# A gated layer's gate and value evacuated over 512 columns, and its input's transposing transfers begun on SyncE

## The chip, the cores and the metric

The kernel runs on one core of a Trainium2 chip. The metric is the time of one execution on the device, in microseconds (us). Times inside an execution are counted from the start of the profiled span.

## What is computed

Three layers, one after the other, over 4 x 768 tokens of 384 features (8 heads of 48):

```python
for t in range(S):                                   # attention with a decaying state
    y[:, :, t] = einsum('bhd,bhde->bhe', rt, state + einsum('bhd,bhe->bhde', u * kt, vt))
    state = wt[:, :, :, None] * state + einsum('bhd,bhe->bhde', kt, vt)
x = y.transpose(0, 2, 1, 3).reshape(B * S, H * D)    # 3072 x 384
x = (1 / (1 + exp(-(x @ w_gate))) * (x @ w_val)) @ w_out      # gated layer, width 1536
h = x @ w_in
return (h * tanh(log1p(exp(h)))) @ w_out2                     # width 2048
```

## The kernel before

All matmuls of the two layers run in half precision with each operand split in a high and a low part, three products for one (high by high, high by low, low by high). Weights come from memory as 64-bit words and are decoded on the chip (`decode`, `decode_early`) into those two parts.

The tokens go in 12 pairs of attention steps, p = 0 to 11, each a block of 256 tokens (`NT`); step j = 2p + e makes one half of a block. `step(j)` computes the attention's rows on TensorE (tile `yp`, L728), splits them into high and low (`xs`, lines 212 and 215) and brings them, turned, into `xt[p]`, the input of the gated layer. For p = 0 and 1 TensorE turns them (`flip_x`, L747) and ScalarE and VectorE copy them out of PSUM (`put`); from p = 2 on two transposing transfers do it (`send`, L762), begun on ScalarE's queue, one for the high and one for the low part. They make 40 transfers in all.

`gate(p, f)` handles 128 of the 1536 inner features (f = 0 to 11). TensorE makes nine matmuls of 256 columns with the gate weights and nine with the value weights (L880), into the two halves of one PSUM bank (tile `gv`, tags pg0 to pg3; three of them for p = 0, four later). Four steps then evacuate the bank: ScalarE's sigmoid of the gate half (L891), VectorE's product with the value half, in place (L896), ScalarE's high part of it into `gt` (L908), VectorE's rest into `gt` (L911). After the last one the bank is free. `out1(p, c, part)` multiplies the finished `gt` of a block with the output weights (L943), in parts that are strewn among the gates of the next block; its result `xo` goes to memory (`x2d`, L979) and is read back for the second layer (`h`, L1053; `o`, L1168), which begins after the last block.

The order of work on every engine is a planner's. Each piece is added with its engine, an estimated cost in us, what it reads and what it writes; the planner computes a latest start for each from the end back, walks forward taking on each engine the ready piece with the earliest latest start, and writes the program in the order of the planned begins. Engines then run their own lists in that order and wait on semaphores. On TensorE the gates come in the order of p and f; attention's matmuls go in between. SyncE's list holds the loads of raw weights (L267), of `blk` (L449) and `v` (L471) for attention, the stores of `x2d` (L979) and the loads of `x2` (L1032).

The lines that carry the four steps' planned costs before are these:

```python
        add("act", 0.34, sigmoid, [ps, "table1"], [sg])
        add("dve", 0.35, product, [sg], [ps])
        ...
            add("act", 0.34, high, [ps, *room], [(*G, 0)])
        ...
        add("dve", 0.35, rest, [ps, (*G, 0)], [(*G, 1)])
```

Of the kernel before, what the change touches and what calls it, by code (L numbers as in the profile page):

```python
# [7 lines left out]
F32 = mybir.dt.float32  # L8
# [3 lines left out]
AF = mybir.ActivationFunctionType  # L12
# [19 lines left out]
NT = 256  # L32
# [3 lines left out]
SW = 256.0  # L36
SX = 64.0
# [8 lines left out]
COLD = 1.9  # L46
# [17 lines left out]
class Plan:  # L64
# [11 lines left out]
    def add(self, eng, cost, fn, reads=(), writes=(), lat=SEM, burst=False):  # L76
        t = Task()
        t.cost = eng if isinstance(eng, dict) else {eng: cost}
        t.fn, t.lat, t.burst = fn, lat, burst
        t.rank = len(self.tasks)  # L80
        t.deps = set()
        for k in reads:
            if k in self.writer:
                t.deps.add(self.writer[k])
        for k in writes:
            if k in self.writer:
                t.deps.add(self.writer[k])
            t.deps.update(self.readers.pop(k, ()))
        for k in reads:
            self.readers.setdefault(k, []).append(t)  # L90
        for k in writes:
            self.writer[k] = t
        self.tasks.append(t)
# [66 lines left out]
def mixer_moe_kernel(  # L160
# [12 lines left out]
    nc = tc.nc  # L173
    PS = bass.MemoryType.PSUM
    plan = Plan()
    add = plan.add
# [6 lines left out]
    mp = ctx.enter_context(tc.tile_pool(name="mp", bufs=1))  # L183
    pg = ctx.enter_context(tc.tile_pool(name="pg", bufs=1, space=PS))
# [20 lines left out]
    def attn(eng, cost, fn, reads=(), writes=(), lat=SEM, burst=False):  # L205
        add(eng, cost, fn, [*reads, "attention"], writes, lat, burst)
# [51 lines left out]
    def next_pg(n=4):  # L258
        npg[0] += 1
        return ("pg", npg[0] % n)  # L260
# [449 lines left out]
    def step(j):  # L710
        p, e = divmod(j, 2)
# [46 lines left out]
        def send(_):  # L758
            if e == 0:
                new_xt()  # L760
            for i in range(2):
                nc.scalar.dma_start_transpose(  # L762
                    out=xt[p][:, i, :, 128 * e : 128 * e + 128], in_=xss[j][:, i]
                )

# [20 lines left out]
        reads = [(*xs, 0), (*xs, 1)]  # L786
        room = [("xt", p % 2, 0, 0)] * e
        if p < 2:

            tbank = next_at()  # L790
            attn("pe", 0.6, flip_x, [*reads, "eye"], [tbank])
            attn("act", 0.48, lambda on: put(on, 0), [tbank, *room], [("xt", p % 2, e, 0)])
            room = [("xt", p % 2, 0, 0)]
            attn("dve", 0.48, lambda on: put(on, 1), [tbank, *room], [("xt", p % 2, e, 1)])
        else:
            new = [("xt", p % 2, e, i) for i in range(2)]
            attn("act", 0.15, send, [*reads, *room], new, lat=2.8)
        if j + 1 == NJ:
            return

# [47 lines left out]
        cold = COLD if j < 4 else 1.0  # L848
# [8 lines left out]
    gps = {}  # L857
    gt = {}
    sgs = {}
    ops = {}  # L860
    xos = {}
    nsg = [0]
    nxo = [0]
    w2 = {}

    def gate(p, f):
        ps = next_pg(4 if p else 3)
        sg = ("sig", nsg[0] % 3)
        nsg[0] += 1
        G = ("gt", p % 2, f)  # L870
        fs = slice(128 * f, 128 * f + 128)

        def sums(o):
            if o == 0:
                gps[p, f] = pg.tile([128, 2, NT], F32, tag=f"pg{ps[1]}", name=f"gv{p}_{f}")
            w = (wgs, wvs)[o]
            n = 0
            for a, c in ((0, 0), (0, 1), (1, 0)):
                for kc in range(KC):
                    nc.tensor.matmul(  # L880
                        gps[p, f][:, o],
                        w[:, a, kc, fs],
                        xt[p][:, c, kc, :],
                        start=(n == 0),
                        stop=(n == 3 * KC - 1),
                    )
                    n += 1

        def sigmoid(e):
            sgs[p, f] = mp.tile([128, NT], F32, tag=f"sig{sg[1]}", name="sig")  # L890
            nc.scalar.activation(  # L891
                out=sgs[p, f], in_=gps[p, f][:, 0], func=AF.Sigmoid, scale=1.0 / (SW * SX)
            )

        def product(e):
            nc.vector.scalar_tensor_tensor(  # L896
                out=gps[p, f][:, 1],
                in0=gps[p, f][:, 1],
                scalar=SG / (SW * SX),
                in1=sgs.pop((p, f)),  # L900
                op0=ALU.mult,
                op1=ALU.mult,
            )

        def high(e):
            if f == 0:
                gt[p] = mp.tile([128, 2, NF1, NT], F16, tag=f"gt{p % 2}", name=f"gt{p}")
            nc.scalar.copy(out=gt[p][:, 0, f], in_=gps[p, f][:, 1])  # L908

        def rest(e):  # L910
            nc.vector.tensor_tensor(  # L911
                out=gt[p][:, 1, f],
                in0=gps[p, f][:, 1],
                in1=gt[p][:, 0, f],
                op=ALU.subtract,
            )

        x = [("xt", p % 2, e, i) for e in range(2) for i in range(2)]
        for o in range(2):
            w = [(("wg", "wv")[o], f, a) for a in range(2)]  # L920
            cold = COLD if p == 0 and f < 3 else 1.0
            add("pe", 0.99 * cold, lambda e, o=o: sums(o), [*x, *w, "gates"], [ps])
        add("act", 0.34, sigmoid, [ps, "table1"], [sg])
        add("dve", 0.35, product, [sg], [ps])
        room = [("gt", p % 2, "tile")]
        if f:
            add("act", 0.34, high, [ps, *room], [(*G, 0)])
        else:
            add("act", 0.34, high, [ps], [(*G, 0), *room])
        add("dve", 0.35, rest, [ps, (*G, 0)], [(*G, 1)])  # L930

    def out1(p, c, part):
        bank = "po2" if p > NP - 3 and (KC * p + c) % 2 else "po"
        cs = slice(128 * c, 128 * c + 128)
        fr = range(3 * part, 3 * part + 3)

        def sums(e):
            if part == 0:
                pool = w2["po"] if bank == "po2" else po
                ops[p, c] = pool.tile([128, 512], F32, tag="po", name=f"o1{p}_{c}")  # L940
            for f in fr:
                for n, (a, g) in enumerate(((0, 0), (1, 0), (0, 1))):
                    nc.tensor.matmul(  # L943
                        ops[p, c][:, :NT],
                        wos[:, a, f, cs],
                        gt[p][:, g, f, :],
                        start=(f == 0 and n == 0),
                        stop=(f == NF1 - 1 and n == 2),
                    )

        reads = [("gt", p % 2, f, a) for f in fr for a in range(2)]
        reads.append(("gt", p % 2, "tile"))
        reads += [("wo", f // 2, a) for f in fr for a in range(2)]
        if bank == "po2":
            reads.append("open")
        add("pe", 0.99, sums, [*reads, "outs"], [bank])
        if part < 3:
            return
        n = nxo[0]
        nxo[0] += 1  # L960
        xo = ("xo", n % 3)

        def new():
            xos[n] = mp.tile([128, 2, NT], F16, tag=f"xo{n % 3}", name="xo")

        split(
            xo,
            lambda: ops[p, c][:, :NT],
            lambda: xos[n][:, 0],
            lambda: xos[n][:, 1],  # L970
            SX / (SW * SG),
            0.35,
            [bank],
            new,
        )
        add(
            "sp",
            0.4,
            lambda e: nc.sync.dma_start(out=x2d[p, c], in_=xos[n]),  # L979
            [(*xo, 0), (*xo, 1)],  # L980
            [("x2d", p, c)],
            lat=2.0,
        )
# [322 lines left out]
    for p in range(NP):  # L1306
        for f in range(NF1):
            if p + 1 < NP:
                if f == YPOS[0]:
                    tail1(p + 1)  # L1310
                if f == YPOS[1]:
                    tail2(p + 1)
                    if p + 2 < NP:
                        cells[p + 2] = fine(p + 2)
                    else:
                        tail_end()
            if f == 0 and p >= NP - 1:
                load_x2(0)
                load_x2(1)
            gate(p, f)  # L1320
            if p > 0:
                for part in PARTS[f % 4] if p > 2 else [f % 4]:
                    out1(p - 1, f // 4, part)

            if f == 3 and p > 1 and (p + 2, 2) in late:
                late.pop((p + 2, 2))()
            if f == 11 and (p + 3, 1) in late:
                late.pop((p + 3, 1))()
# [73 lines left out]
```

## Time and profile before

| | us |
|---|---|
| median of three runs | 967.01 (963.94 to 968.82) |
| the profiled execution, its own time | 966.59 |
| its span, first to last instruction | 964.9 |
| TensorE busy in the span | 895.1 |
| VectorE busy | 662.0 |
| ScalarE busy | 497.1 |
| GpSimd busy | 490.6 |

The engines are named PE (TensorE matmuls), PEld (its weight loads), DVE (VectorE), ACT (ScalarE), POOL (GpSimd) and SP (SyncE). A q behind an engine's name means its queue, where transfers are issued. L880 is line 880 of the kernel. In a row of a group, the part before the bar names line, engine, operation and tiles; behind it stand busy time, the mean of one instruction, and the idle time of the engine just before, with what ended it.

### The profile page before, as it was taken

To read this page: it belongs to the slowest core of one execution; us is meant where nothing else is said; L and a number is where in the kernel's file an instruction comes from. 1 tells how busy PE (TensorE), PEld (TensorE's weight loads), DVE (VectorE), ACT (ScalarE), POOL (GpSimd) and SP (SyncE) were. 2 spreads that over 40 slices of the span, in tenths; PEclk is the share of its full clock that TensorE was granted. 3 is DMA by queue.
4 is the path that set the end of the run, shared out by engine and by line. 5 is a ranking of instruction groups with operands and counts; after the bars stand their busy time and mean duration, and the time that the engine had idled before them with its cause. 6 is when DMAs were issued, how large, how long until landed. Compare 5 with 4: busy or idle time off the path is not lost.

```text
span 964.9 us, 29600 instructions
## 1 busy us (share of the span) xinstructions
PE 895.1 (93%) x12808; PEld 715.3 (74%) x12808; DVE 662.0 (69%) x1202; ACT 497.1 (52%) x1191; POOL 490.6 (51%) x534
## 2 busy tenths in 40 slices
PE   0567899999999999999999999999999999999998
PEld 0455678888888888888888787657767676776788
DVE  7889976767676857686778798875565655556541
ACT  2757864343525253443436566775565655656540
POOL 7999832626454536546374365654343443444330
PEclk9988899999999999999999999999999999999999
DMA  9445842322232223232222760010100102000000
GB/s 316 143 139 165 261 116 75 67 69 69 68 56 69 75 70 80 49 75 59 61 53 78 190 206 12 8 44 1 37 30 10 58 1 66 2 9 26 1 34 34
DMA packets 56467, 71.92 MB, mean 75 GB/s; under 512 B 20752, under 2 KB 37648, under 8 KB 56208
## 3 DMA queue, kind: packets, MB, share of 16 engines
q1 hardware_dynamic: 39696, 66.09, 23.3%
q10 hardware_dynamic: 16640, 3.94, 2.1%
q8 instruction: 100, 1.64, 0.7%
q14 instruction: 31, 0.25, 0.1%
HBM read 56.64 MB, written 9.44 MB: 68 GB/s over the span
## 4 chain that ended last, share of the span: by engine, by line
PE 71%; DVE 13%; ACT 7%; POOL 4%; ACTq 2%; issue 2%; DMA 1%; SPq 0%; DVEq 0%; POOLq 0%
PE gv L880 20%; PE h L1053 19%; PE o L1168 17%; PE o L943 10%; PE yp L728 3%; ACT X L655 2%; DVE X L655 2%; ACTq L762 2%; ACT KK L697 2%; DVE A L506 1%; PE kp L824 1%; POOL sum_wp L332 1%; PE lp L638 1%; DVE gt L911 1%; POOL pt L486 1%
## 5 line engine op out<-in xcount | busy, mean ns | idle before, releaser
L1053 PE MATMUL h<-x,wis 128*128 128x512 f16 x864 | 199.9, 379 | 1.3 <-DVE gt L911 1.3
L880 PE MATMUL gv<-xt,wgs 128*128 128x256 f16 x1296 | 165.0, 277 | 14.7 <-DVE gt L911 14.1
L486 POOL TENSOR_TENSOR blk<-blk 128x384 f32<-128x384 f32 (+2 forms) x139 | 127.6, 931 | 99.4 <-DMA blk<-rkw 71.7
L943 PE MATMUL o<-gt,wos 128*128 128x256 f16 x1296 | 165.3, 273 | 2.2 <-DVE xo L215 2.0
L1087 POOL TENSOR_TENSOR sum<-e 128x256 f32<-128x256 f32 x96 | 71.6, 746 | 185.8 <-ACT e L1064 185.7
L880 PE MATMUL gv<-xt,wvs 128*128 128x256 f16 x1296 | 163.9, 276 | 1.9 <-DVE wvs L306 1.2
L880 PEld LDWEIGHTS <-wgs 128*128 128x128 f16 x1296 | 125.8, 99 | 33.7 <-issue 15.7
L1053 PEld LDWEIGHTS <-wis 128*128 128x128 f16 x864 | 83.4, 98 | 84.4 <-issue 1.5
L943 PEld LDWEIGHTS <-wos 128*128 128x128 f16 x1296 | 125.9, 98 | 20.6 <-issue 2.9
L880 PEld LDWEIGHTS <-wvs 128*128 128x128 f16 x1296 | 125.1, 99 | 20.4 <-DVE wvs L306 1.5
L486 POOL TENSOR_TENSOR pt<-blk 128x384 f32<-128x384 f32 x93 | 105.5, 1159 | 45.0 <-DMA blk<-rkw 41.7
L891 ACT ACTIVATE sig<-gv 128x256 f32<-128x256 f32 x144 | 53.6, 385 | 118.0 <-PE gv L880 110.5
L1064 ACT ACTIVATE e<-h 128x512 f32<-128x512 f32 x96 | 57.3, 597 | 84.0 <-PE h L1053 83.0
L911 DVE TENSOR_TENSOR gt<-gv,gt 128x256 f16<-128x256 f32 x144 | 58.8, 418 | 53.9 <-ACT gt L908 52.5
L908 ACT CAST gt<-gv 128x256 f16<-128x256 f32 x144 | 52.7, 371 | 76.1 <-DVE gv L896 54.4
L896 DVE SCALAR_TENSOR_TENSOR gv<-gv,sig 128x256 f32<-128x256 f32 x144 | 60.8, 432 | 30.3 <-ACT sig L891 29.7
L1168 PE MATMUL o<-wps,gt 128*128 128x192 f16 x612 | 74.0, 246 | 0.0
L655 ACT COPY X<-lp 24x64 f32<-24x64 f32 x174 | 44.6, 257 | 39.0 <-DVE X L655 28.4
L1106 DVE SCALAR_TENSOR_TENSOR gt<-e,gt 128x256 f16<-128x256 f32 x41 | 27.5, 683 | 49.6 <-ACT gt L1101 49.6
L506 DVE TENSOR_REDUCE A<-pt 128x32 f32<-128x768 f32 (+1 forms) x60 | 51.4, 863 | 12.3 <-POOL pt L486 12.3
L1168 PE MATMUL o<-wps,wgs 128*128 128x192 f16 x498 | 59.4, 246 | 0.0
L1168 PE MATMUL o<-wps,wos 128*128 128x192 f16 x456 | 57.1, 246 | 0.0
(106 smaller groups left out, 1506.7 us busy)
## 6 DMA issues: line engine op xcount, KB each, us to landing
v<-vt SPq DMA_DIRECT2D x96, 96.0 KB, 3.2
blk<-rkw SPq DMA_DIRECT2D x22, 384.0 KB, 3.5
raw_wi<-wi SPq DMA_DIRECT2D x8, 768.0 KB, 5.5
raw_wp<-wo SPq DMA_DIRECT2D x8, 768.0 KB, 6.1
blk<-rkw SPq DMA_DIRECT2D x11, 512.0 KB, 3.7
raw_wg<-wg SPq DMA_DIRECT2D x6, 768.0 KB, 6.2
raw_wv<-wv SPq DMA_DIRECT2D x6, 768.0 KB, 6.1
raw_wo<-wo SPq DMA_DIRECT2D x6, 768.0 KB, 4.8
```

The source lines that it names most:

```text
L486: engines[e].tensor_tensor(out=pv, in0=a, in1=b, op=ALU.mult)
L506: nc.vector.tensor_reduce(out=cell(), in_=shape(pts.pop(n)), op=ALU.add, axis=AX.X)
L655: put(out=xp[p][rs, xs, t:], in_=lps[p, e][rs, :, c : c + C - t])
L880: nc.tensor.matmul(gps[p, f][:, o], w[:, a, kc, fs], xt[p][:, c, kc, :], start=(n == 0), stop=(n == 3 * KC - 1),)
L891: nc.scalar.activation(out=sgs[p, f], in_=gps[p, f][:, 0], func=AF.Sigmoid, scale=1.0 / (SW * SX))
L896: nc.vector.scalar_tensor_tensor(out=gps[p, f][:, 1], in0=gps[p, f][:, 1], scalar=SG / (SW * SX), in1=sgs.pop((p, f)), op0=ALU.mult, op1=A ...
L911: nc.vector.tensor_tensor(out=gt[p][:, 1, f], in0=gps[p, f][:, 1], in1=gt[p][:, 0, f], op=ALU.subtract,)
L943: nc.tensor.matmul(ops[p, c][:, :NT], wos[:, a, f, cs], gt[p][:, g, f, :], start=(f == 0 and n == 0), stop=(f == NF1 - 1 and n == 2),)
L1053: nc.tensor.matmul(hps[r, f], w2["wi"][:, a, kc, fs], x2[r][:, c, kc, :], start=(n == 0), stop=(n == 3 * KC - 1),)
L1064: nc.scalar.activation(out=es[r, f], in_=hps[r, f], func=AF.Mish, scale=ih)
L1087: engines[e].tensor_tensor(out=sums[0][:, n - 1], in0=a(), in1=b(), op=op)
L1168: nc.tensor.matmul(ops2[h, first], home(slots[r, i, name])[:, c, tsl], w2["wp"][:, a, w, i, :], start=(new and n == 0), stop=(n == 3 * NF2 ...
```

## The change

Two neighbouring blocks of 128 features, f = 2i and 2i + 1, now share their banks and their evacuation. One bank takes both gate results, another both value results; sigmoid, product, high part and rest each run once over 2 x 256 = 512 columns. TensorE's order becomes gate 2i, gate 2i + 1 (at f = 2i) and value 2i, value 2i + 1 (at f = 2i + 1), with the parts of `out1` behind each two. The sigmoid reads the gate bank alone. The buffers of the sigmoid's result are two of 512 columns instead of three of 256. The planned costs of the four steps become 0.58 and 0.67. And `send` begins its two transposing transfers on SyncE instead of ScalarE, where the planner counts its 0.15 us as well.

```diff
@@ step
-                nc.scalar.dma_start_transpose(
+                nc.sync.dma_start_transpose(
...
-            attn("act", 0.15, send, [*reads, *room], new, lat=2.8)
+            attn("sp", 0.15, send, [*reads, *room], new, lat=2.8)
@@ gate
-    def gate(p, f):
-        ps = next_pg(4 if p else 3)
-        sg = ("sig", nsg[0] % 3)
+    def gate(p, i):
+        n = 4 if p else 3
+        banks = [next_pg(n) for _ in range(2)]
+        sg = ("sig", nsg[0] % 2)
...
-        def sums(o):
-            if o == 0:
-                gps[p, f] = pg.tile([128, 2, NT], F32, tag=f"pg{ps[1]}", name=f"gv{p}_{f}")
+        def sums(o, h):
+            if h == 0:
+                gps[p, i, o] = pg.tile(
+                    [128, 2, NT], F32, tag=f"pg{banks[o][1]}", name=f"gv{p}_{i}_{o}"
+                )
...
-                        gps[p, f][:, o],
+                        gps[p, i, o][:, h],
...
-            sgs[p, f] = mp.tile([128, NT], F32, tag=f"sig{sg[1]}", name="sig")
+            sgs[p, i] = mp.tile([128, 2, NT], F32, tag=f"sig{sg[1]}", name="sig")
...
-                out=sgs[p, f], in_=gps[p, f][:, 0], func=AF.Sigmoid, scale=1.0 / (SW * SX)
+                out=sgs[p, i], in_=gps[p, i, 0], func=AF.Sigmoid, scale=1.0 / (SW * SX)
...
-            nc.scalar.copy(out=gt[p][:, 0, f], in_=gps[p, f][:, 1])
+            nc.scalar.copy(out=gt[p][:, 0, 2 * i : 2 * i + 2], in_=gps[p, i, 1])
...
+        def fill(o, h):
+            w = [(("wg", "wv")[o], two[h], a) for a in range(2)]
+            cold = COLD if p == 0 and two[h] < 3 else 1.0
+            add("pe", 0.99 * cold, lambda e: sums(o, h), [*x, *w, "gates"], [banks[o]])
+
+        def finish():
+            add("act", 0.58, sigmoid, [banks[0], "table1"], [sg])
+            add("dve", 0.67, product, [sg], [banks[1]])
+            room = [("gt", p % 2, "tile")]
+            if i:
+                add("act", 0.58, high, [banks[1], *room], [G[0]])
+            else:
+                add("act", 0.58, high, [banks[1]], [G[0], *room])
+            add("dve", 0.67, rest, [banks[1], G[0]], [G[1]])
@@ the loop over p and f
-            gate(p, f)
+            if f % 2 == 0:
+                fill, finish = gate(p, f // 2)
+            fill(f % 2, 0)
+            fill(f % 2, 1)
+            if f % 2:
+                finish()
```

## Rows read from the trace of the kernel before

**Rows 1.** The page's first part: busy us, share of the span, instructions.

```profile
PE 895.1 (93%) x12808; PEld 715.3 (74%) x12808; DVE 662.0 (69%) x1202; ACT 497.1 (52%) x1191; POOL 490.6 (51%) x534
```

**Rows 2.** Windows by stage: us, busy PE, PEld, DVE, ACT, POOL, clock, DMA share, GB/s.

```profile
25.00:110.00 85.00, 56.26 (x1232) 44.40 (x1223) 74.86 (x117) 61.35 (x130) 79.30 (x74) 0.89 0.52 168
110.00:560.00 450.00, 439.59 (x8255) 379.14 (x8254) 325.26 (x605) 208.56 (x547) 218.47 (x222) 1.00 0.33 83
...
600.00:964.90 364.90, 361.59 (x2975) 259.86 (x2972) 207.02 (x401) 197.51 (x462) 147.11 (x192) 1.00 0.08 24
```

**Rows 3.** Waits of TensorE, 25 to 110 us: total, times, longest.

```profile
PE gv L880 <- DVE gt L911: 13.0, 4, 4.5
```

**Rows 4.** Waits of TensorE, 110 to 600 us.

```profile
PE yp L728 <- DVE s L835: 3.0, 8, 0.9
...
PE h L1053 <- DVE gt L911: 1.3, 1, 1.3
...
PE gv L880 <- DVE gt L911: 1.1, 1, 1.1
```

**Rows 5.** Timeline of TensorE at the end of the ramp: start, length, [idle before].

```profile
105.95 2.08 PE L880 MATMUL gv<-xt,wgs 128*128 128x256 f16 x9 [2.43 <-DVE gt L911]
...
109.75 1.49 PE L880 MATMUL gv<-xt,wgs 128*128 128x256 f16 x6
```

**Rows 6.** Timeline of VectorE there.

```profile
101.20 1.77 DVE L306 TENSOR_TENSOR wvs<-word_wv,wvs 128x768 f16<-128x768 f32 x1
...
105.51 0.40 DVE L911 TENSOR_TENSOR gt<-gv,gt 128x256 f16<-128x256 f32 x1
```

**Rows 7.** Timeline of ScalarE there.

```profile
107.61 0.47 ACT L756 COPY xt<-xp 128x384 f16<-128x384 f16 x1
```

**Rows 8.** Groups by line and shape.

```profile
L896 DVE SCALAR_TENSOR_TENSOR gv<-gv,sig 128x256 f32<-128x256 f32 x144 | 60.8, 432 | 30.3 <-ACT sig L891 29.7
...
L911 DVE TENSOR_TENSOR gt<-gv,gt 128x256 f16<-128x256 f32 x144 | 58.8, 418 | 53.9 <-ACT gt L908 52.5
L1064 ACT ACTIVATE e<-h 128x512 f32<-128x512 f32 x96 | 57.3, 597 | 84.0 <-PE h L1053 83.0
...
L891 ACT ACTIVATE sig<-gv 128x256 f32<-128x256 f32 x144 | 53.6, 385 | 118.0 <-PE gv L880 110.5 <-DMA xt<-xs 3.7 <-DVE X L644 3.5
...
L908 ACT CAST gt<-gv 128x256 f16<-128x256 f32 x144 | 52.7, 371 | 76.1 <-DVE gv L896 54.4 <-DMA xt<-xs 11.7 <-issue 9.7
...
L215 DVE SCALAR_TENSOR_TENSOR xs<-yp,xs 128x384 f16<-128x384 f32 x24 | 13.2, 550 | 3.7 <-ACT xs L212 3.7
```

**Rows 9.** Timeline of TensorE in blocks 6 and 7.

```profile
378.74 2.13 PE L880 MATMUL gv<-xt,wgs 128*128 128x256 f16 x18
```

**Rows 10.** The line of the transposing transfers: min/median/max in ns.

```profile
L762 ACTq DMA_TRANSPOSE xt<-xs x40: 1193/1206/3263, 132.3 to 548.1; - x40
```

**Rows 11.** Timeline of ScalarE around the sends of block 7.

```profile
366.41 2.51 ACTq L762 DMA_TRANSPOSE xt<-xs  x2
```

**Rows 12.** Transfers issued in 355 to 370 us: KB, median us to landing.

```profile
xt<-xs ACTq DMA_TRANSPOSE x4, 4.5
```

**Rows 13.** Timeline of ScalarE at the last send.

```profile
546.55 2.79 ACTq L762 DMA_TRANSPOSE xt<-xs  x2
```

**Rows 14.** Transfers issued in 545 to 549 us.

```profile
raw_wp<-wo SPq DMA_DIRECT2D x1, 768.0 KB
x2d<-xo SPq DMA_DIRECT2D x1, 128.0 KB, 5.6
xt<-xs ACTq DMA_TRANSPOSE x2, 5.8
```

**Rows 15.** Timeline of TensorE at block 11's first gate.

```profile
557.54 1.69 PE L880 MATMUL gv<-xt,wgs 128*128 128x256 f16 x14
```

**Rows 16.** Transfers of the whole span.

```profile
x2d<-xo SPq DMA_DIRECT2D x36, 128.0 KB, 1.7
```

**Rows 17.** Waits of SyncE's queue.

```profile
SPq L979 <- DVE xo L215: 190.8, 24, 12.2
```

More of the change, by code (lines that the diff above doesn't have):

```diff
@@ L864, in mixer_moe_kernel @@
     w2 = {}
-    def gate(p, f):
-        ps = next_pg(4 if p else 3)
-        sg = ("sig", nsg[0] % 3)
+    def gate(p, i):
+        n = 4 if p else 3
+        banks = [next_pg(n) for _ in range(2)]
+        sg = ("sig", nsg[0] % 2)
         nsg[0] += 1
-        G = ("gt", p % 2, f)
-        fs = slice(128 * f, 128 * f + 128)
-        def sums(o):
-            if o == 0:
-                gps[p, f] = pg.tile([128, 2, NT], F32, tag=f"pg{ps[1]}", name=f"gv{p}_{f}")
+        two = range(2 * i, 2 * i + 2)
+        G = [("gt", p % 2, i, a) for a in range(2)]
+        def sums(o, h):
[3 more added lines that the diff above has]
+                )
             w = (wgs, wvs)[o]
+            fs = slice(128 * (2 * i + h), 128 * (2 * i + h) + 128)
             n = 0
@@ L896, in product @@
             nc.vector.scalar_tensor_tensor(
-                out=gps[p, f][:, 1],
-                in0=gps[p, f][:, 1],
+                out=gps[p, i, 1],
+                in0=gps[p, i, 1],
                 scalar=SG / (SW * SX),
-                in1=sgs.pop((p, f)),
+                in1=sgs.pop((p, i)),
                 op0=ALU.mult,
@@ L905, in high @@
         def high(e):
-            if f == 0:
+            if i == 0:
                 gt[p] = mp.tile([128, 2, NF1, NT], F16, tag=f"gt{p % 2}", name=f"gt{p}")
-            nc.scalar.copy(out=gt[p][:, 0, f], in_=gps[p, f][:, 1])
+            nc.scalar.copy(out=gt[p][:, 0, 2 * i : 2 * i + 2], in_=gps[p, i, 1])
         def rest(e):
             nc.vector.tensor_tensor(
-                out=gt[p][:, 1, f],
-                in0=gps[p, f][:, 1],
-                in1=gt[p][:, 0, f],
+                out=gt[p][:, 1, 2 * i : 2 * i + 2],
+                in0=gps[p, i, 1],
+                in1=gt[p][:, 0, 2 * i : 2 * i + 2],
                 op=ALU.subtract,
@@ L918, in gate @@
         x = [("xt", p % 2, e, i) for e in range(2) for i in range(2)]
[L919 to L930, printed above, removed]
+        def fill(o, h):
[11 more added lines that the diff above has]
+            add("dve", 0.67, rest, [banks[1], G[0]], [G[1]])
+        return fill, finish
     def out1(p, c, part):
@@ L949, in sums @@
                     )
-        reads = [("gt", p % 2, f, a) for f in fr for a in range(2)]
+        reads = [("gt", p % 2, f // 2, a) for f in fr for a in range(2)]
         reads.append(("gt", p % 2, "tile"))
```

## The prediction

> **What bounds the kernel now.** I read the page first, then the windows by stage, the waits of TensorE by stage, and the timeline at the one place where stages change hands. The page puts TensorE at 895.1 of 964.9 us [rows 1]. The windows say where the rest lies [rows 2]. From 600 us on TensorE has work without a pause until the last drain (361.59 of 364.9 us); nothing that the diff touches runs there. From 110 to 560 us it is busy for 439.59 of 450 us, at full clock. From 25 to 110 us it is busy for only 56.26 of 85 us, at 0.89 of the clock, while VectorE has 74.86 and GpSimd 79.30 of the 85. So the span is a ramp of about 110 us, set by VectorE, GpSimd and ScalarE (attention of the first blocks, decoding of the first weights), and then a line of matmuls with few holes. A change to the gate's evacuation can shorten the ramp or fill the holes, and nothing else.
>
> How much is in each? In the ramp TensorE waited 13.0 us in four places for a gate bank, each time for the last VectorE step on it (L911) [rows 3]. From 110 to 560 us it is idle for 10.4 us in all [rows 2], and from 110 to 600 us only 1.1 us (gate) and 1.3 us (the first h) of its waits are for L911; the largest item, 3.0 us in eight pieces, is attention's (L835) [rows 4]. The end of the ramp is in the timeline: the last wait for a bank ends at 105.95, block 1 begins at 109.75, and from there the matmuls are dense [rows 5]. Just before, VectorE wrote the last value weights at 101.20 to 102.97, and the L911 that freed the bank came only at 105.51, 2.5 us of other steps later [rows 6]. ScalarE wrote the last of block 1's input at 107.61 to 108.08 [rows 7].
>
> **The change part by part.** *Evacuation.* 144 times four steps of 256 columns become 72 times four of 512. Before: sigmoid 385 ns, product 432, high part 371, rest 418 [rows 8]. No row has these steps at 512. The sigmoid is nearest to the activation at 512, 597 ns. VectorE's scalar_tensor_tensor went from 432 at 256 to 550 at 384 columns, 0.92 ns a column, so 668 at 512; the rest by the same slope 654; the high part by the sigmoid's, (597 - 385) / 256 = 0.83 ns, 583 [rows 8]. Bounds for VectorE: no less than the 550 of 384 columns, no more than two of 256. With these values a pair costs ScalarE 597 + 583 = 1.18 us where it cost 2 x (385 + 371) = 1.51, and VectorE 668 + 654 = 1.32 where it cost 2 x (432 + 418) = 1.70: 0.33 and 0.38 us less. Over 72 pairs that is 24 us of ScalarE and 27 us of VectorE. After 110 us these engines are off the path (VectorE 325, ScalarE 209 of 450 us [rows 2]), so it is worth nothing there by itself. In the ramp block 0's six pairs take 2.3 us off VectorE and 2.0 off ScalarE. VectorE is 88% busy there, so what it does last comes nearly that much sooner: I take -2.0 us; bounds 0 (GpSimd, 93% busy, sets the end) and -2.3.
>
> *Banks.* Before, a bank held gate and value of one block and came free after all four steps. Now a gate bank is free after the sigmoid, which need no longer wait for the value passes. With block 0's three banks TensorE could issue six passes before it needed a rest (L911); now eight, since the fourth bank use, value of pair 1, only needs the first sigmoid. Of the 13.0 us, the first three waits lie where the weights set the pace anyway: with banks free TensorE would next wait for weights that came at 102.97. Only the last, 2.43 us [rows 5], touches the end of the ramp. Half of it may be what was saved already by VectorE's shorter queue: I take -1.0 us; bounds 0 and -13.0. In the later blocks, with four banks, the time for a value bank stays ten passes (gate, value and out1 parts between one use and the next, as before), some 1 us each (two in 2.13 [rows 9]), 10 us; the chain in it is product, high, rest, 2.0 us plus hand-overs, where it was 1.6. It costs nothing; the cover is 7 us wide, and without it the 0.4 us of difference would be paid for each of the 72 pairs. At the seam to the second MLP the first h takes a bank that now waits for a sigmoid only: of the 1.1 + 1.3 us [rows 4] I take -2.0; bounds 0 and -2.4.
>
> *Longer steps in front of attention.* A VectorE step of 0.67 instead of 0.43 us can hold an attention step up 0.25 us more. The waits of yp for L835 came eight times [rows 4]: at most +2 us; the steps are half as many, so it may also give 2 back. I take 0.
>
> *The transposing transfers.* Forty issues of 1.2 us each [rows 10] leave ScalarE's queue, 48 us; the longest held it for 3.26. No wait of TensorE in rows 4 comes from that, so its worth is 0; what it gives ScalarE is slack. On SyncE the issues stand in its order: behind them are loads of v and blk and the stores of x2d. SyncE's own issues are short and it mostly waits; a v load 2.4 us later fills a buffer that is needed three steps on. The transfer itself: in block 7 the second of the pair that began at 366.41 [rows 11] was issued some 1.25 us later, half of its 2.51, and landed a median 4.5 us after that [rows 12], so about 372.2; block 7's first gate ran at 378.74 [rows 9]: 6.5 us to spare. The tightest is block 11: issued from 546.55 to 549.34 [rows 13], landing 5.8 us after issue beside a 768 KB load [rows 14], so by about 554, and the first gate at 557.54 [rows 15]: 3.5 us or more. A store that SyncE issued right behind that load took 5.6 us [rows 14] against a median of 1.7 [rows 16], 3.9 us more; the transposes already carry 1.3 of this (5.8 against a median 4.5), so behind the load they would lose about 2.6 us more, within the 3.5. I take 0; bounds 0 and +5.
>
> The store's 5.6 us shows requests of one queue served in their order. The Trainium skill, "DMA: Bandwidth & Descriptors", section on queues, rings and completion order, says this: SyncE and ScalarE own a ring each on every DMA engine, and a ring is taken in order. It speaks against the move, since transposes lose a ring of their own. By that rule block 11's transposes land after the raw load ahead of them, as the store did, and the sum stays the same as by the rows; it would grow only with two loads ahead, where 2 x 3.9 us exceed the 3.5 to spare.
>
> **Sum.** The profiled execution took 966.59 us (span 964.9 and 1.7 around it), 0.4 under the median 967.01. -2.0 - 1.0 - 2.0 = -5.0: 961.6, as a median 962.0.
>
> **Rivals.** *Hidden.* The ramp ends when GpSimd's and the attention's work ends, and 2 us on VectorE are used up by other steps that stand ready; block 1's input at 108.08 [rows 7] comes as late as before. For it: GpSimd at 93%. Against: the last steps before 105.95 are VectorE's. Then only the seam's 0 to 2.4 us are won: 964.6 to 967.
>
> *The ramp gives more.* All four bank waits go, and TensorE has block 0 done as the weights come: -13.0 - 2.4 = 951.6. Against: 102.97 for the last weights leaves at most some 7 us (109.75 - 102.97) unless the decoding itself moves up.
>
> *SyncE's order is the new wait (slower).* SyncE stands at x2d's store 24 times, up to 12.2 us [rows 17]. If a send falls behind such a wait, the input lands up to 12 us late; it decides from 6.5 us on in a usual block (3.5 in block 11), and the excess, 5.7 us for 12.2, is paid in each block where it happens: one block 973, two 978. Against: the planner orders SyncE by the time at which things are ready, and store and send follow from the same TensorE order; a planned time would have to be off by over 6.5 us.
>
> *The new order of the ramp is dearer.* Different costs reorder the steps on VectorE and GpSimd; the waits there may grow as well as shrink. A step of 2 us (a flip) ahead of the last weights at two places: +4, with nothing saved 971.
>
> **Chances.** As forecast (958 to 964): 0.38. Ramp gives more (951 to 958): 0.14. Hidden (964 to 969): 0.28. SyncE's order: 0.08. Dearer ramp: 0.12, half of it beyond 0.5%. A change of 0.5%, 4.8 us, is about what can be told from none; the forecast lies just at it, so its chance is parted: faster 0.14 + 0.31 = 0.45; slower 0.08 + 0.06 = 0.14; the same 0.41. The range leaves out a tenth at each end: 953 to 972; by the likeliest alone 958 to 964.
>
> **What would show it.** Sigmoid, product, high and rest 72 times each at about 0.60, 0.67, 0.58 and 0.65 us, and VectorE's sum down by some 27 us. The first dense gate of block 1 at about 106.5 instead of 109.75, fewer waits for the rest step in the ramp; busy time of TensorE from there unchanged. No wait of TensorE for the first h. The transposes on SyncE's queue at 1.2 us, landing at 4 to 6 us, and no gate passes waiting for them. I am wrong if block 1 begins no sooner, if gates wait for transposes, or if TensorE is idle for more than 10.4 us from 110 to 560.

## The result

The changed kernel takes 957.55 us (median of five runs, 956.97 to 960.65) against 965.83 before in the same comparison: a ratio of 0.9919, with a 95% interval of 0.9898 to 0.9939. It is faster by about 8 us, where 5 were forecast. The profiled execution took 960.65 us, the slowest of the five, so its trace shows 5.9 us of the gain (966.59 before) and says nothing of the rest.

The page's first part answers to [rows 1], the windows by stage to [rows 2]:

```profile
PE 892.5 (93%) x12808; PEld 713.3 (74%) x12808; DVE 653.7 (68%) x1057; ACT 483.5 (50%) x1055; POOL 483.1 (50%) x527
```

```profile
25.00:110.00 85.00, 58.75 (x1219) 46.27 (x1220) 78.20 (x108) 63.38 (x124) 80.37 (x74) 0.89 0.53 172
110.00:560.00 450.00, 441.05 (x8353) 381.38 (x8351) 320.18 (x488) 196.24 (x432) 215.44 (x223) 1.00 0.32 87
...
600.00:958.90 358.90, 355.68 (x2942) 256.65 (x2939) 201.14 (x392) 192.08 (x447) 143.19 (x187) 1.00 0.08 24
```

The shape is the same: a ramp, then a dense line. VectorE's sum falls by only 8 us although its two steps on the banks got 19 us shorter (119.6 to 100.5). Added up one by one, its instructions last 727.5 us before and 710.0 now, 17.5 less: busy time counts a stretch in which two overlap only once, and there are 145 fewer to overlap. Some other steps grew or came over from GpSimd, whose sum fell by 7.5. The groups by line and shape answer to [rows 8]:

```profile
L900 DVE SCALAR_TENSOR_TENSOR gv<-gv,sig 128x512 f32<-128x512 f32 x72 | 51.1, 709 | 57.8 <-ACT sig L895 30.6 <-PE gv L884 26.6
L915 DVE TENSOR_TENSOR gt<-gv,gt 128x512 f16<-128x512 f32 x72 | 49.4, 686 | 15.6 <-ACT gt L912 15.4
...
L895 ACT ACTIVATE sig<-gv 128x512 f32<-128x512 f32 x72 | 43.0, 597 | 72.8 <-PE gv L884 72.4
L912 ACT CAST gt<-gv 128x512 f16<-128x512 f32 x72 | 42.1, 584 | 94.5 <-DVE gv L900 94.2
```

TensorE's waits from 25 to 110 us and from 110 to 600 us answer to [rows 3] and [rows 4]:

```profile
PE gv L884 <- DVE gt L915: 4.7, 2, 3.1
PE gv L884 <- POOL wvs L306: 3.0, 2, 2.2
PE gv L884 <- ACT xt L756: 3.0, 1, 3.0
```

```profile
PE gv L884 <- DVE gt L915: 3.0, 3, 1.3
PE yp L728 <- DVE RD L623: 2.5, 6, 0.6
PE o L952 <- DVE xo L215: 2.2, 1, 2.2
...
PE yp L728 <- DVE s L835: 1.1, 2, 0.9
```

In the ramp the waits for a bank fell from 13.0 to 4.7 us, but others took their place: the last weights (L306) and block 1's input (L756). Later, attention's L835 fell from 3.0 to 1.1, and the banks' last step (L911, now L915) rose from 1.1 to 3.0.

To see where a gain lies I cut every run at the first gate of block 2, of block 10 and of block 11 and at the first h, as the timeline of TensorE shows them, all in us:

| run | block 2 begins | blocks 2 to 9 | block 10 | block 11 | first h to end | span |
|---|---|---|---|---|---|---|
| before | 155.8 | 355.7 | 46.1 | 39.3 | 368.0 | 964.9 |
| changed | 154.7 | 350.0 | 44.9 | 41.3 | 368.0 | 958.9 |
| send alone moved | 154.6 | 349.6 | 47.7 | 38.8 | 368.2 | 958.9 |
| pairing alone | 157.4 | 350.0 | 46.3 | 41.0 | 368.0 | 962.7 |
| send moved, ScalarE held | 155.4 | 358.9 | 46.6 | 40.7 | 368.2 | 969.9 |
| before, costs lowered | 158.5 | 360.3 | 47.0 | 40.0 | 368.3 | 974.2 |
| before, costs as measured | 153.6 | 350.6 | 45.5 | 41.8 | 368.0 | 959.5 |
| changed, costs as measured | 154.0 | 347.2 | 43.6 | 38.3 | 368.0 | 951.1 |
| changed, costs 0.68, 0.70 | 151.8 | 346.2 | 45.4 | 37.1 | 368.0 | 948.5 |
| the same, send on ScalarE | 150.9 | 346.2 | 44.3 | 38.3 | 368.0 | 947.8 |
| send moved, before's costs as measured | 153.9 | 347.4 | 47.2 | 35.8 | 368.2 | 952.5 |
| changed, block 0 unpaired | 154.2 | 350.9 | 44.9 | 39.8 | 368.0 | 957.8 |
| changed, block 0 alone paired | 155.0 | 349.7 | 46.6 | 39.3 | 368.0 | 958.6 |
| changed, block 11 unpaired | 153.2 | 349.4 | 46.1 | 39.6 | 368.0 | 956.3 |

So in the profiled execution the change gave 1.1 us up to block 2, 5.7 in blocks 2 to 9, 1.1 in block 10, lost 2.0 in block 11 and left the rest alone. Most of it came from the stage for which nothing was forecast. Each row is one execution, and executions of one kernel differ by up to 8 us; what several rows repeat is safer than a single difference of 1 or 2. In blocks 2 to 9 TensorE's idle time fell from 5.9 to 2.5 us (355.7 less 349.8 busy; 350.0 less 347.6), and its busy time by 2.3 with the same 6691 matmuls.

### The profile page after: what moved, and what is told of

Read it like the earlier page. It is cut to its first block, busy times and chain, and to the rows that moved or that the text cites. A ratio compares the mean times of both kernels' runs of the same rounds, so it can differ in the third digit from the quotient of the medians.

```text
span 958.9 us, 29333 instructions
## 1 busy us (share of the span) xinstructions
PE 892.5 (93%) x12808; PEld 713.3 (74%) x12808; DVE 653.7 (68%) x1057; ACT 483.5 (50%) x1055; POOL 483.1 (50%) x527
## 4 chain that ended last, share of the span: by engine, by line
PE 78%; DVE 9%; POOL 6%; ACT 3%; DMA 2%; issue 2%; SPq 0%; DVEq 0%; ACTq 0%; POOLq 0%
PE gv L884 22%; PE h L1062 19%; PE o L1177 17%; PE o L952 13%; PE yp L728 3%; POOL pt L486 2%; POOL blk L486 2%; PE kp L824 2%; DVE X L655 1%; ACT X L655 1%; DMA blk<-rkw 1%; DMA xt<-xs 1%; DVE gt L915 1%; DVE word_wp L292 1%; DVE RD L623 1%
## 5 line engine op out<-in xcount | busy, mean ns | idle before, releaser
L884 PE MATMUL gv<-xt,wgs 128*128 128x256 f16 x1296 | 169.0, 277 | 10.3 <-DVE gt L915 4.7
L884 PE MATMUL gv<-xt,wvs 128*128 128x256 f16 x1296 | 168.5, 276 | 6.4 <-DVE gt L915 3.0
L486 POOL TENSOR_TENSOR blk<-blk 128x384 f32<-128x384 f32 (+3 forms) x139 | 125.0, 917 | 92.5 <-DMA blk<-rkw 72.4
L884 PEld LDWEIGHTS <-wgs 128*128 128x128 f16 x1296 | 123.5, 99 | 30.0 <-ACT wgs L397 5.8
L486 POOL TENSOR_TENSOR pt<-blk 128x384 f32<-128x384 f32 (+1 forms) x93 | 107.5, 1181 | 54.3 <-DMA blk<-rkw 52.7
L900 DVE SCALAR_TENSOR_TENSOR gv<-gv,sig 128x512 f32<-128x512 f32 x72 | 51.1, 709 | 57.8 <-ACT sig L895 30.6
L912 ACT CAST gt<-gv 128x512 f16<-128x512 f32 x72 | 42.1, 584 | 94.5 <-DVE gv L900 94.2
L895 ACT ACTIVATE sig<-gv 128x512 f32<-128x512 f32 x72 | 43.0, 597 | 72.8 <-PE gv L884 72.4
L915 DVE TENSOR_TENSOR gt<-gv,gt 128x512 f16<-128x512 f32 x72 | 49.4, 686 | 15.6 <-ACT gt L912 15.4
L1177 PEld LDWEIGHTS <-gt 128*128 128x128 f16 x612 | 52.9, 98 | 3.3
```

The costliest lines, as they stand in the source:

```text
L486: engines[e].tensor_tensor(out=pv, in0=a, in1=b, op=ALU.mult)
L884: nc.tensor.matmul(gps[p, i, o][:, h], w[:, a, kc, fs], xt[p][:, c, kc, :], start=(n == 0), stop=(n == 3 * KC - 1),)
L895: nc.scalar.activation(out=sgs[p, i], in_=gps[p, i, 0], func=AF.Sigmoid, scale=1.0 / (SW * SX))
L900: nc.vector.scalar_tensor_tensor(out=gps[p, i, 1], in0=gps[p, i, 1], scalar=SG / (SW * SX), in1=sgs.pop((p, i)), op0=ALU.mult, op1=ALU.mult,)
L912: nc.scalar.copy(out=gt[p][:, 0, 2 * i : 2 * i + 2], in_=gps[p, i, 1])
L915: nc.vector.tensor_tensor(out=gt[p][:, 1, 2 * i : 2 * i + 2], in0=gps[p, i, 1], in1=gt[p][:, 0, 2 * i : 2 * i + 2], op=ALU.subtract,)
```

## The experiments

Two theories stood after the traces. Theory A: before, the two issues of a send held ScalarE; what came late behind them reached TensorE, and the move ended that, while pairing gave its own share. Theory B: all is pairing. A third, C, came from the kernel's make: the planner had other costs to plan with, and its new order, not shorter steps, gave the gain. The path that A names can be read before at the first send for block 7 (TensorE is in block 6's gates then), in the timelines of ScalarE, VectorE and TensorE:

```profile
356.56 3.73 ACTq L762 DMA_TRANSPOSE xt<-xs  x2
360.33 0.37 ACT L908 CAST gt<-gv 128x256 f16<-128x256 f32 x1 [3.45 <-issue]
```

```profile
360.74 0.42 DVE L911 TENSOR_TENSOR gt<-gv,gt 128x256 f16<-128x256 f32 x1 [2.54 <-ACT gt L908]
361.08 1.01 DVE L835 TENSOR_TENSOR s<-kp,s 128x384 f32<-128x384 f32 x2
```

```profile
361.68 0.27 PE L728 MATMUL yp<-s,RD 64*32 64x48 f32 x2 [0.87 <-DVE s L835]
```

The cast waits for the queue, VectorE's rest for the cast, the attention's join L835 stands behind the rest in VectorE's order, and TensorE's yp waits for L835. This is not the only place: each of yp's waits for L835 from 150 to 510 us ends 1.4 to 1.9 us after a send's last issue, and in the whole run the idle time before L908 that ended with a send's issue is 21.4 us in eight pieces ([rows 8]: "DMA xt<-xs" and "issue").

**One part at a time.** The send alone moved:

```diff
-                nc.scalar.dma_start_transpose(
+                nc.sync.dma_start_transpose(
-            attn("act", 0.15, send, ...)
+            attn("sp", 0.15, send, ...)
```

> The kernel before with the transposing transfers alone moved to SyncE. Theory A (two gains): before, a pair of issues held ScalarE for up to 3.7 us, the high part (L908) and VectorE's L911 came late behind it, and VectorE's L835 and with it yp on TensorE; the move takes TensorE's waits for L835 in the blocks 4, 6 and 8 away (2.5 of 3.0 us) and some waits of its weight loads, the ramp stays (block 1 begins near 109.7): about 962, ratio 0.996. Theory B (all is the pairing): L835's waits stay, ratio 1.000.

961.46 us, ratio 0.9959 (0.9945 to 0.9972). Blocks 2 to 9 took 349.6 us. TensorE's waits from 150 to 510 us are one row, where before had also 2.6 us for L835:

```profile
PE yp L728 <- DVE RD L623: 2.4, 4, 0.7
```

Theory A's number; B falls. No cast waits for a send's issue any more, as the group's idle time shows:

```profile
L908 ACT CAST gt<-gv 128x256 f16<-128x256 f32 x144 | 52.5, 370 | 40.3 <-DVE gv L896 39.5
```

(The planner's order changes a little with the move; the run with the hold put back, below, keeps that order.) The pairing alone (the changed kernel with the two lines above undone):

> The changed kernel with the transposing transfers put back on ScalarE. Theory A: block 1 begins near 106, TensorE's waits for L835 return in some of the blocks 4 to 8 with a late L912 and L915 before them: about 962, ratio 0.996. Theory B: as the changed kernel, 958, ratio 0.992.

961.35 us, ratio 0.9954 (0.9936 to 0.9971). The time is A's, the trace is not: no wait for L835 is left from 150 to 510 us, though ScalarE is still held (timeline of ScalarE, then of VectorE):

```profile
355.00 3.29 ACTq L762 DMA_TRANSPOSE xt<-xs  x2
361.78 0.59 ACT L912 CAST gt<-gv 128x512 f16<-128x512 f32 x1 [6.24 <-DVE gv L900]
```

```profile
357.00 1.02 DVE L835 TENSOR_TENSOR s<-kp,s 128x384 f32<-128x384 f32 x2 [1.06 <-PE kp L824]
...
361.05 0.70 DVE L900 SCALAR_TENSOR_TENSOR gv<-gv,sig 128x512 f32<-128x512 f32 x1 [2.56 <-PE gv L884]
```

No cast falls into the hold here, so L835 waits for nothing but TensorE. In the whole run L912 waits for products alone:

```profile
L912 ACT CAST gt<-gv 128x512 f16<-128x512 f32 x72 | 42.0, 583 | 90.5 <-DVE gv L900 90.3
```

Whether that is because casts are half as many or because the pairing has another order was not separated. Either part removes the same 5.7 to 6.1 us of blocks 2 to 9; together they remove them once. That the two ratios multiply to 0.9913, near the 0.9919 of both, therefore comes from the other stages, of which single traces show only part. Between the pairing alone and the changed kernel (961.35 and 957.55 us) the traces differ by 2.7 us up to block 2 and by 1.4 in block 10; in block 1, TensorE's granted clock was 0.92 against 0.95.

**The hold put back.** The send on SyncE, with copies on ScalarE in its old place:

```diff
+            for i in range(2):
+                for n in range(3):
+                    nc.scalar.copy(out=holds[0], in_=xss[j][:, i])
```

> The kernel before with the transposing transfers on SyncE, and in their old place ScalarE copies the high part three times and the low part three times into a buffer that nothing reads, about 0.45 us each, the last three only once VectorE has written the low part: ScalarE is held as long as by the two issues, and the planner's order stays that of the send alone moved. Theory A (the hold on ScalarE reaches TensorE by way of L908, L911 and L835): the waits of yp for L835 return, the blocks 2 to 9 take about 355 us instead of 349.6, the time about 965. Rival (the move gained by the other order of the program, not by a free ScalarE): they stay at 349.6, the time at 961.5.

970.74 us, ratio 1.0046 (1.0028 to 1.0063), blocks 2 to 9 in 358.9 us. Its first send for block 7 repeats the pattern, in the timelines of ScalarE and VectorE, with TensorE's waits from 150 to 510 us:

```profile
356.99 3.23 ACT L768 COPY hold<-xs 128x384 f16<-128x384 f16 x6
360.12 0.36 ACT L912 CAST gt<-gv 128x256 f16<-128x256 f32 x1
```

```profile
360.52 0.42 DVE L915 TENSOR_TENSOR gt<-gv,gt 128x256 f16<-128x256 f32 x1 [2.24 <-ACT gt L912]
360.87 1.01 DVE L839 TENSOR_TENSOR s<-kp,s 128x384 f32<-128x384 f32 x2
```

```profile
PE yp L729 <- DVE s L839: 5.4, 14, 0.6
PE yp L729 <- DVE RD L624: 3.0, 5, 0.7
```

(L839 is L835 with four lines above it.) The hold alone, in the order of the send alone moved, brings the waits back and more: theory A's path is shown. Its size is not: the time overshoots A's 965. The copies hold ScalarE for 3.2 us at nearly every send, where before a pair of issues held it for 2.5 to 4.6, in the median 2.7.

**The planner's costs.** Before, with nothing but its planned costs lowered to half of a pair's:

```diff
-        add("act", 0.34, sigmoid, ...)      # high likewise
+        add("act", 0.29, sigmoid, ...)
-        add("dve", 0.35, product, ...)      # rest likewise
+        add("dve", 0.335, product, ...)
```

> The kernel before with nothing changed but the planned costs of the four steps, to half of what the changed kernel plans for a pair (0.29 and 0.335). Theory C (the planner's other order gives the gain, not shorter steps): 0.994 or less. Theory A: within 2 us of before, ratio 0.998 to 1.002; how far it strays tells what the order of the ramp alone is worth.

974.34 us, ratio 1.0095 (1.0075 to 1.0116): slower, by a new order alone. TensorE's waits from 150 to 510 us:

```profile
PE yp L728 <- DVE RD L623: 6.6, 6, 1.8
PE yp L728 <- DVE s L835: 1.6, 4, 1.0
```

Theory C in its first form falls, for these costs make it worse; but A's "within 2 us" falls as well. The other way round, the changed kernel planned with twice the costs of before:

```diff
-            add("act", 0.58, sigmoid, ...)      # high likewise
+            add("act", 0.68, sigmoid, ...)
-            add("dve", 0.67, product, ...)      # rest likewise
+            add("dve", 0.70, product, ...)
```

> The changed kernel with planned costs of a pair twice those of before (0.68 and 0.70), so that the planner sees no saving while the steps run as short as before in the changed kernel. Theory C: the gain falls to half or less, ratio 0.996 or more. Theory A: within 2 us of the changed kernel, 0.990 to 0.994.

949.80 us, ratio 0.9836 (0.9823 to 0.9848): neither theory's number. From 150 to 510 us TensorE has no wait at all in the list, each of the blocks 4 to 9 takes 43.26 us, and the steps themselves are as long as in the changed kernel (705 and 685 ns on VectorE). From this came theory D: the planner loses time where it holds VectorE to be faster than it is. Before, with costs as measured:

```diff
-        add("act", 0.34, sigmoid, ...) / add("dve", 0.35, product, ...) / 0.34 high / 0.35 rest
+        add("act", 0.385, sigmoid, ...) / add("dve", 0.43, product, ...) / 0.37 high / 0.42 rest
```

> The kernel before with the planned costs of the four steps set to their measured durations (0.385, 0.43, 0.37, 0.42 instead of 0.34, 0.35, 0.34, 0.35). Theory D (the planner loses time where it thinks VectorE faster than it is; costs that are nearer the measured ones remove waits for L835 and L623): faster than before, 960 or less. Rival (costs only shuffle the order, up or down by chance): anywhere from 957 to 975, with no fewer waits for L835 in blocks 2 to 9.

963.55 us, ratio 0.9978 (0.9961 to 0.9995), with waits for L835 and L623 of 1.2 and 0.8 us in blocks 2 to 9 instead of 2.6 and 2.2: the direction is D's, but the time did not reach its 960. Here the send still holds ScalarE and nothing is paired (L908 waits 14.7 us in six pieces for the issues, against 21.4 in eight), and yet blocks 2 to 9 take 350.6 us. So what the hold costs depends on the order behind it, and a third edit, of costs alone, removes most of the same 5.7 us. The changed kernel with costs as measured:

```diff
-            0.58 sigmoid, 0.67 product, 0.58 high, 0.67 rest
+            0.60 sigmoid, 0.71 product, 0.585 high, 0.69 rest
```

> The changed kernel with planned costs as measured (0.60, 0.71, 0.585, 0.69 instead of 0.58, 0.67, 0.58, 0.67). Theory D: like the costs of 0.68 and 0.70, about 950, with the waits for L623 in blocks 4 to 9 gone; VectorE's costs are what matters. Rival: anywhere from 950 to 962.

952.87 us, ratio 0.9867 (0.9843 to 0.9891), 4.7 us under the changed kernel; one kind of wait, 0.6 us for L623, is left in blocks 2 to 9. D's direction again, but costs above the measured ones on ScalarE did better still, so that true costs are best is not shown. Unpaired with costs as measured and the send moved (the edits of the first and the fifth run together):

> Unpaired as before, the send on SyncE, planned costs of the four steps as measured (0.385, 0.43, 0.37, 0.42). It stands to the paired kernel with measured costs (952.9) as the send alone moved stands to the changed kernel. Theory A with D: both gains add, so 963.5 - 4 = about 959.5, and pairing is worth some 6 us more with honest costs. Rival (honest costs make pairing needless): 953 or less.

955.70 us, ratio 0.9907 (0.9893 to 0.9922): no worse than the changed kernel (0.9898 to 0.9939), without any pairing. The move is worth some 7 us with these costs (0.9978 to 0.9907), more than the 4 expected, and in the traces it is mostly block 11 (41.8 to 35.8 us). Pairing is worth the step from 0.9907 to 0.9867 here, some 4 us, less than the 6 expected. And the paired kernel with 0.68 and 0.70, its send put back on ScalarE:

> Paired, planned costs 0.68 and 0.70, the send on ScalarE. Theory A (either the move or the pairing takes the waits for L835 away, they do not add in blocks 2 to 9): blocks 2 to 9 within 1 us of 346.2, the time 950 to 952. Rival (the move is worth 4 us by itself whatever else): 954, and waits for L835 in blocks 2 to 9 again.

950.05 us, ratio 0.9845 (0.9832 to 0.9858), blocks 2 to 9 in 346.2 us without a wait. As theory A says of pairing, the move is worth nothing here that can be told: the intervals of 0.9836 and 0.9845 overlap. With the changed kernel's own costs it was worth 0.9954 to 0.9919, outside blocks 2 to 9.

**The ramp and the seam.** Block 0 unpaired, all others paired (`PAIRED` says which blocks are; `gate1` has two buffers for the sigmoid's result where `gate` before had three):

```diff
+            if p not in PAIRED:
+                gate1(p, f)                      # gate() of before
+            else:
                 if f % 2 == 0:
                     fill, finish = gate(p, f // 2)
```

> The changed kernel, but block 0 is evacuated unpaired as before. Theory R1 (in the ramp the pairing gains by itself: shorter VectorE queue and banks that come free sooner): that gain goes and the time rises to that of the send alone moved, about 961, with TensorE's waits for L911 in block 0 back to about 12 us. Theory R2 (the ramp's difference has another source): 957.5, as the changed kernel.

958.15 us, ratio 0.9931 (0.9918 to 0.9943), not to be told from 0.9919, though the ramp's waits for a bank came back (10.5 us from 25 to 110 us). Block 2 began at 154.2 against 154.7 in the changed kernel: R1's 961 falls. Block 0 alone paired:

> The changed kernel with block 0 alone paired, all others unpaired. Theory R1: the ramp's gain stays, blocks 2 to 9 take 349.6 as with the send alone moved, so about 957.5. Theory R2: no better than the send alone moved, 961.5.

960.02 us, ratio 0.9946 (0.9933 to 0.9958), between the two theories and within the interval of the send alone; block 2 began at 155.0. The two runs put the pairing of block 0 at some 1.2 us each (0.9931 against 0.9919, 0.9946 against 0.9959), which the intervals do not tell from nothing. Block 11 alone unpaired:

> The changed kernel, but the last block, 11, is evacuated unpaired as before (256 columns, bank by bank). Theory E (pairing itself makes block 11 longer: value banks of 512 columns wait for L915 behind VectorE's decoding of the last weights, 3.0 us): block 11 goes from 41.3 back to about 39.3 us and the time down by 2, to about 955.5. Rival (decoding sets block 11's length, however evacuated): no change, 957.5.

959.69 us, ratio 0.9935 (0.9913 to 0.9957). Block 11 took 39.6 us instead of 41.3, as theory E says, but the waits for a bank did not go (3.9 us, one of 3.0), and the time did not fall. In other runs block 11 was paired as well and took 41.0 us (pairing alone), 39.8 (block 0 unpaired), 38.3 (costs as measured) and 37.1 (0.68 and 0.70); unpaired it took 35.8 to 41.8. So pairing by itself does not make it long. What decides its length stays unsettled.

## Why the prediction was right, and where it was not

The time, 957.55, lies in the range, just below the likeliest part of 958 to 964, and the sign is right. That is partly luck: of the sum's terms the seam gave nothing and the ramp a third, and the largest gain came from a stage and a term that were set to 0.

*Evacuation.* The sizes held: sigmoid 597 for 597 ns, high 584 for 583, product 709 for 668, rest 686 for 654, the last two 5 to 6% dearer. A pair costs VectorE 1.40 us, not 1.32, and VectorE's sum fell by 8 us where 27 were to show it.

*The ramp, -3.0.* This failed. Block 1 did begin at 106.05 instead of 109.75, as forecast, and the wait for banks fell by 8.3 us. But the marker was bad: by block 2 only 1.1 us was left. Block 0 now leaves 64 of attention's matmuls (L638, 0.89 us before) to block 1. And after a stretch in which TensorE mostly waited (busy for 2.3 and 2.5 us from 100 to 106 us), its granted clock was 0.50 (1.2 GHz) from 106 to 111 us in both traces. Before, two passes of block 0 ran at it (one is in [rows 5]); now they are block 1's:

```profile
106.05 2.08 PE L884 MATMUL gv<-xt,wgs 128*128 128x256 f16 x9 [2.98 <-ACT xt L756]
107.92 2.12 PE L884 MATMUL gv<-xt,wvs 128*128 128x256 f16 x9
109.84 1.73 PE L884 MATMUL gv<-xt,wgs 128*128 128x256 f16 x9
```

So at 109.8 us TensorE was two passes ahead, an estimated 2 us at the full clock (18 matmuls took 2.12 us at 95.53), and less the 0.9 us of the 64 matmuls that is the 1.1 left, not 3.7. The wait for block 1's input (L756), which the rival "hidden" had named, now ends the ramp in place of the wait for a bank. With block 0 unpaired nothing measurable was lost. The step that failed is "Only the last, 2.43 us [rows 5], touches the end of the ramp": behind the waits for banks stood those for the last weights and the input.

*The seam, -2.0.* Nothing was left of it. The first h waits no more (1.3 us to nothing). The gates do: they waited 3.0 us for L915 instead of 1.1 for L911, out1 2.2 for xo instead of 0.9, and block 11 got longer by 2.0. The step that failed is "the cover is 7 us wide". It counted the chain's own length, not what stands in front of L915 on a VectorE that is decoding the last weights. (Unpaired, block 11 had such waits too, 3.9 us.) The timeline of VectorE in the changed kernel, before a wait of 1.27 us:

```profile
575.38 0.69 DVE L900 SCALAR_TENSOR_TENSOR gv<-gv,sig 128x512 f32<-128x512 f32 x1
575.98 0.78 DVE L346 CAST wps<-word_wp 128x384 f16<-128x384 f32 x1
576.68 1.61 DVE L332 TENSOR_TENSOR wps<-word_wp,wps 128x192 f16<-128x192 f32 x2
578.21 0.68 DVE L915 TENSOR_TENSOR gt<-gv,gt 128x512 f16<-128x512 f32 x1
```

From the product's start to the rest's, with one cast of 0.6 us on ScalarE between them, it took 2.8 us.

*The send on ScalarE, 0.* The sentence "No wait of TensorE in rows 4 comes from that" was wrong. The waits for L835 in [rows 4] came of that hold, two engines further, in the order that this kernel had; I had followed the wait to VectorE and not asked why VectorE's step was late. These waits, which the move and the pairing each remove, are most of the 5.7 us of blocks 2 to 9. The listed waits for L835 there are only 2.6 us; yp's weight loads waited for it too (4.9 us in 14 pieces from 150 to 510 us before, none in the changed kernel). The two overlap: 2.2 of the 4.9 us lie in stretches that TensorE counts as busy, which fits the 2.3 us by which its busy time fell.

*The send on SyncE, 0.* This held. The issues stayed at 1.2 us, and the landing became shorter, a median 3.1 instead of 3.9 us over all forty:

```profile
L762 SPq DMA_TRANSPOSE xt<-xs x40: 1178/1202/2511, 132.2 to 541.0; - x40
...
DMA to landing us min/median/max: 2.3/3.1/8.0
```

At the last send the transfers landed late, as [rows 14] had let expect, and the gates still did not wait (transfers issued in 538 to 545 us, then TensorE's timeline). Two raw loads were issued right ahead of it, from 536.11 to 539.71, the case in which the prediction let the sum grow:

```profile
raw_wp<-wo SPq DMA_DIRECT2D x1, 768.0 KB, 6.4
x2d<-xo SPq DMA_DIRECT2D x1, 128.0 KB, 6.0
xt<-xs SPq DMA_TRANSPOSE x2, 7.5
```

```profile
549.66 1.15 PE L884 MATMUL gv<-xt,wgs 128*128 128x256 f16 x9
```

The second was issued at about 541.0, so it was there some 1 us before the first gate, where 3.5 had been to spare. That it landed late because it stood behind the loads in one queue is not shown: before, a pair sent from ScalarE's own queue beside two such loads took 7.4 us (533 to 540 us).

*The order.* The rival "new order of the ramp is dearer" looked for the planner's reorder in the ramp and gave it 4 us. It reaches the whole gated layer: costs alone put the kernel before at 0.9978 or at 1.0095, and brought the changed one from 0.9919 to 0.9836.

What stays open: which stage holds the 1.8 to 3.7 us by which the other four executions are shorter than the profiled one, what sets the length of block 11, and how much of each gain is the edit's own and how much the order that the planner makes of it.

## What to carry to other kernels

When a busy matmul engine waits for a step, ask what made that step late, and follow it through every engine's order to the first queue that stood still; a transfer's issue on a computing engine can cost its neighbours even where that engine is half idle (ScalarE was busy for 52% here). Two edits that remove the same wait do not add in its stage, so undo each alone before crediting either. Where a planner orders the work, measure what its costs alone do before reading a gain as that of the instructions: here costs of 0.68 and 0.70 gave the shortest time, 949.8 us, nearly as much again as the whole change.

## What was not expected of the hardware

Transposing transfers landed sooner from the queue that also carries the loads (median 3.1 us) than from ScalarE's (3.9 us). This repeats with whichever engine sends: 2.9 and 3.0 us in the send alone and with costs 0.68 and 0.70, from SyncE; 3.9 and 3.6 us in the pairing alone and with those costs, from ScalarE. No run tells why. Issuing one took the queue 1.2 us on either engine, in the median, against 0.34 us for a store of x2d.
